# Four moves in the order of work of a fused attention and mixer kernel: k.v split about its denominators, blocks closed in pairs, w2's loads behind another event, S4 earlier

## The chip, the cores and the metric

The kernel runs on one core of one Trainium2 chip. The metric is the device time of an execution in microseconds (us); the median of three runs before the change is 292.44 us, from 292.41 to 292.49.

The engines are called as the profile calls them: PE is TensorE's matmuls and PEld its weight loads, DVE is VectorE, ACT is ScalarE, POOL is GpSimd and SP is SyncE, which issues most DMA transfers. L684 is line 684 of the kernel before the change.

## What is computed

Cosine-weighted linear attention over 8 batches, 8 heads, 576 tokens of 64 features, and behind it a mixer over tokens of rank 32 and a two-layer perceptron over channels (512 to 2048 to 512).

```python
q_p, k_p = phi(q), phi(k)               # relu, times cos and sin of the position: 128 features
kv = einsum('bhsf,bhsd->bhfd', k_p, v)
z = sum(k_p, axis=2)
x = einsum('bhsf,bhfd->bhsd', q_p, kv) / (einsum('bhsf,bhf->bhs', q_p, z) + 1e-6)
# x goes to (batch, token, 512)
u = x + ((x.T @ U) @ V).T               # U: 576 x 32, V: 32 x 576
out = u + relu(u @ w_ch1) @ w_ch2
```

## The kernel before

**Tiles.** The 576 tokens of a batch are four chunks of 128 (c = 0 to 3) and a tail of 64 (c = 4); the tails of two batches share one tile of 128 rows. All products run in bf16 and add up in PSUM in fp32. PSUM's banks go by tags that rotate: "g" has three (`G3` in the code), "T" (`T1`) and the pair "oA", "oB" one each, "X" a double one.

**Order.** The order is written by hand: each engine has one queue of instructions, in the order in which the program emits them, and an instruction that waits holds back all that is behind it on its engine. Batch 0's attention comes first, by functions of its own. Behind it stands a list of slots (`lay`, `lay_all`): each is one unit of TensorE work of some 0.9 us, and `beside` and `todo` put thunks behind given slots (other engines' work, the attention of the next batch, loads). For an even and an odd batch in turn the slots are 16 units of the first product (`first_units`: u @ w_ch1 and relu) and then the second product; batch 0's second product is 16 plain units (`g2_part`, L755), the others' are 14 half steps (`second_units`, `w_part`).

**Batch 0's attention.** q's chunks are turned into features by DVE and ACT (`q_prep`, L307 and L305), transposed on TensorE (`qtr_mm`, L386, into the three "g" banks and oA, oB) and copied to `q_pT` (`qtr_evac`, L114 on ACT and L116 on DVE): chunk 0 by DVE, 1 by ACT, 3 and the tail by ACT later. Chunk 2 is copied by DVE inside `first_chain`. k's features follow (`k_prep`), with their sums z as products with ones (`z_mm`, L1178). Then `first_chain` (L1232 to L1282):

- DVE casts v into `v0` in two casts of two heads and one of four, casts z into `z_sb`, and copies q^T's chunk 2 between them.
- `kv_unit(b, 0)` (L341) multiplies heads 0 to 3 (20 products) into a "g" bank; ACT evacuates them to `kv_sb`. Then `den_mm` (L1186): 40 products of 12 columns give the denominators of all chunks; DVE adds 1e-6 and takes the reciprocal (L421, L422).
- `xh_mm` (L1194) gives x before division for a chunk's four heads, `xh_norm` (L1203, DVE) and `xh_norm_act` (L1226, ACT) divide. The second four heads follow `kv_unit(b, 1)`.
- `a_mm` (L457) is x.T @ U for two of the four blocks of 128 channels at a time, in column groups of 32; it reads `x_of(b, c)` of all five chunks. A cast puts it into `A_sb`.
- u^T, block by block: `open_mm` (L1217) transposes x's four chunks into a bank, and `uTd_mm` (L557) "closes" it by adding A times V, one product of 512 columns on a row group of 32. `uTd_evac` casts it to `uT`. Blocks 0 and 1 are opened and closed one after the other; blocks 2 and 3 behind the second `a_mm`, with two of batch 0's first-layer products ahead of their closing (`g1_open`, L701) and four behind.

**Loads.** SP issues q, k and v of the next batches in order, behind one-element copies that hold it until something is done. POOL issues w_ch1 in four loads, then a copy `mark` that reads a piece of batch 1's k (L1326) and so waits until it has landed, then w_ch2 in four (L108). SP's `gate` on w2's second load (L1341) stands ahead of batch 2's loads. Batch 1's k.v (L341, slots 16 and 17) reads casts of v that DVE makes in slots 14 and 15 (`v_half`).

**Second product of batches 1 to 7.** It is done by seven block products instead of eight, with sums of blocks of w2 (`T`) and of the relu output (`S1`, `S2`, `S3`, `S4`; `hid_form`, L830, each in two halves). `w_part(b, n)` is half step n: 8 pairs of products on one of four banks. Steps in order of n / 2: 0 plain, 1 with S2, 2 with S1, 3 with S3, 4 plain, 5 with S4 (into the bank of step 2), 6 plain. The second halves of S1 and S2 are made behind half step 0, S3's behind 2, S4's behind 4. After odd half steps, DVE and POOL take the banks up (L874): behind step 1, DVE adds it to `w_sum`, DVE makes one piece of the output tile `o_sb` and POOL two more; behind steps 2 to 6, DVE adds the bank to its piece.

Of the kernel before, what the change touches and what calls it, by code (L numbers as in the profile page):

```python
# [10 lines left out]
FP32 = mybir.dt.float32  # L11
BF16 = mybir.dt.bfloat16
# [5 lines left out]
def kernel(  # L18
# [93 lines left out]
    def cast(eng, o, i):  # L112
        if eng is nc.scalar:
            nc.scalar.activation(out=o, in_=i, func=AF.Copy, bias=0.0, scale=1.0)  # L114
        else:
            eng.tensor_copy(out=o, in_=i)  # L116
# [216 lines left out]
    def kv_unit(b, hg, tag, bufs, eng=None):  # L333
        if b not in kv_sb:
            kv_sb[b] = pool.tile([P, H, E], BF16, tag="kv", bufs=2, name="kv")
        n = D if b == 0 else E
        acc = bank([P, 4, n], FP32, tag, bufs, "kv_ps")
        for i in range(4):
            h = hg * 4 + i
            for c in range(5):  # L340
                nc.tensor.matmul(  # L341
                    out=acc[:, i, :],
                    lhsT=k_p[b][:, c, h, :] if c < 4 else k_tl[:, h, :],
                    rhs=v0[:, h, c, :] if b == 0 else vx_of(b, c, h),
                    start=(c == 0),
                    stop=(c == 4),
                )
        cast(eng or V_, kv_sb[b][:, hg * 4 : hg * 4 + 4, 0:n], acc)

    def kv_pair(b, tag, bufs):  # L350
        kv_sb[b] = pool.tile([P, H, E], BF16, tag="kv", bufs=2, name="kv")
# [39 lines left out]
    def qtr_evac(b, c, eng, t):  # L391
        if c < 4:
            cast(eng, q_pT[b][:, c, :, :], t)
        else:
            cast(eng, q_tlT[:, :, tail(b)], t[:, :, 0:P:2])
# [156 lines left out]
    def uTd_evac(b, d, eng):  # L552
        cast(eng, uT[b][:, d, :, :], uT_ps[b, d])
# [289 lines left out]
    def w_part(b, n):  # L843
        step, half = divmod(n, 2)
        lhs, rhs, to = (
            (lambda: hid_block(b, 0, 0), w2_block(0, 0), 0),
            (lambda: s_forms[b, 2], T[1], 1),
            (lambda: s_forms[b, 1], T[0], 2),
            (lambda: s_forms[b, 3], T[2], 3),
            (lambda: hid_block(b, 1, 0), w2_block(1, 0), 0),  # L850
            (lambda: s_forms[b, 4], w2_block(1, 1), 2),
            (lambda: hid_block(b, 1, 1), T[3], 3),
        )[step]
        lhs = lhs()
        opens = step < 4
        if opens and half == 0:
            tag, bufs = T1 if to == 0 else G3
            w_ps[to] = bank([P, DM], FP32, tag, bufs, f"w_ps{to}")
        res = w_ps[to].rearrange("p (g n) -> p g n", g=2)
        for k_ in range(half * 4, half * 4 + 4):  # L860
            for g in range(2):
                nc.tensor.matmul(  # L862
                    out=res[:, g, :], lhsT=lhs[:, k_, g * P : g * P + P], rhs=rhs[:, k_, :],
                    start=(opens and k_ == 0 and g == 0),
                    stop=(k_ == KB - 1 and g == 1), skip_group_check=not opens,
                )
        for f in ({0: (4,), 2: (3,)} if b == B - 1 else {0: (1, 2), 2: (3,), 4: (4,)}).get(n, ()):
            hid_form(b, f, 1)
        if half == 0:
            return  # L870
        lo, hi = slice(0, HD), slice(HD, DM)

        def add(eng, o, x, y):
            eng.tensor_tensor(out=o, in0=x, in1=y, op=ALU.add)  # L874

        def by_d(t):
            return t.rearrange("p c (d n) -> p d c n", n=P)

        def u(c0, h):
            return u_bf[b][:, 2 * h : 2 * h + 2, c0 : c0 + 2, :]  # L880

        if step == 0:
            w_sum[b] = pool.tile([P, 2, HD], FP32, tag="w_sum", bufs=1, name="w_sum")
            cast(A_, w_sum[b], res)
        elif step == 1:
            w = w_sum[b]
            o0, o1 = o_alloc(b, 0), o_alloc(b, 1)
            add(V_, w, w, res)
            add(V_, by_d(o1[:, :, hi]), by_d(w), u(2, 1))
            add(G_, by_d(o0[:, :, hi]), by_d(w), u(0, 1))  # L890
            add(G_, by_d(o1[:, :, lo]), by_d(w), u(2, 0))
        elif step == 2 or step == 3:
            o = o_sb[b, 1][:, :, hi]
            add(V_, o, o, res)
        elif step == 4:
            add(V_, by_d(o_sb[b, 0][:, :, lo]), u(0, 0), by_d(res))
        elif step == 5:
            o = o_sb[b, 0][:, :, hi]
            add(V_, o, o, res)
            store_w(b, 0, 0)  # L900
        else:
            o = o_sb[b, 1][:, :, lo]
            add(V_, o, o, res)
            store_w(b, 2, 1)
# [278 lines left out]
    def den_mm(b, d, cs):  # L1183
        for c in cs:
            for h in range(H):
                nc.tensor.matmul(  # L1186
                    out=d[:, c, h, :], lhsT=qT_of(b, c, h),
                    rhs=z_sb[:, h : h + 1].to_broadcast([P, 12]), start=True, stop=True,
                )
# [25 lines left out]
    def open_mm(b, d, t, cs):  # L1215
        for c in cs:
            nc.tensor.matmul(  # L1217
                out=t[:, c, :], lhsT=x_bf[b][:, c, d * P : d * P + P], rhs=ident,
                start=(c == 0), stop=False,
            )  # L1220
# [11 lines left out]
    def first_chain(b, xz, z, v_ps):  # L1232
# [6 lines left out]

        d = xz[:, 1, 0:480].rearrange("p (c h n) -> p c h n", h=H, n=12)  # L1240
        rec = pool.tile([P, 5, H], FP32, tag="rec5", bufs=1, name="rec5")
        for h in (0, 2):
            cast(V_, v0[:, h : h + 2], vst[:, h : h + 2])
        cast(V_, z_sb, z[:, :, 0])
        qtr_evac(b, 2, V_, t_q[2])
        cast(V_, v0[:, 4:H], vst[:, 4:H])
        qtr_evac(b, 4, A_, t_q[4])
        kv_unit(b, 0, *G3, A_)
        cast(A_, V_bf, v_ps.rearrange("r (c p) -> r c p", c=4))
        den_mm(b, d, (0, 1, 3, 2, 4))  # L1250
        recip(rec, d[:, :, :, 0])
        x0 = [xh_mm(b, c, 0, *G3) for c in ORD[0:2]]
        kv_unit(b, 1, *T1, A_)
# [10 lines left out]
        cast(A_, A_of(b)[0:TS, :], a_ps[0:TS, :])  # L1264
        for i, (tag, bufs) in enumerate((OA, OB, T1)):
            uT_ps[b, i] = bank([P, 4, P], FP32, tag, bufs, "uT_ps")
        open_mm(b, 0, uT_ps[b, 0], range(4))
        x1.append(xh_mm(b, ORD[4], 4, *G3))
        for n in range(2, 5):
            xh_norm(b, ORD[n], 4, rec, x1[n])  # L1270
        uTd_mm(b, 0)
        uTd_evac(b, 0, A_)
        open_mm(b, 1, uT_ps[b, 1], range(4))
        uTd_mm(b, 1)
        uTd_evac(b, 1, A_)
        a2 = bank([P, P], FP32, *G3, "a_ps")
        a_mm(b, a2, (2, 3), range(5))
        cast(V_, A_of(b)[TS:P, :], a2[TS:P, :])
# [14 lines left out]
    for c in TL:  # L1293
        q_prep(0, c, FEATS[c])
        qtr_mm(0, c, 0, H, t_q[c])
        keep_warm(1, "X", 1)
    for c, eng in zip(TL[0:2], (V_, A_)):
        qtr_evac(0, c, eng, t_q[c])
    xz = ps.tile([P, 2, 512], FP32, tag="X", bufs=1, name="xz")
    z = xz[:, 0, 0:384].rearrange("p (h n) -> p h n", n=48)  # L1300
# [22 lines left out]
    for h0 in (0, 4):  # L1323
        load_odd(vst, v, 1, h0, h0 + 4)
        load_even(vst, v, 1, h0, h0 + 4)
    G_.tensor_copy(out=mark, in_=kst[0:TS, 3, 4, 0:1])  # L1326
    for n in range(4):
        w2_load(n)
    g1_open(0, (0, 0), (0, 1))
    uTd_close(0, 2, V_)  # L1330
    uTd_close(0, 3, A_)
    g1_open(0, (0, 2), (1, 0), (1, 1), (1, 2))
    q_prep(1, 4, (V_, A_))
    q_prep(1, 0, (V_, V_))


    def at(j, *thunks):
        beside.setdefault(j, []).extend(thunks)

    def gate(src):  # L1340
        nc.sync.dma_start(out=mark2, in_=src)  # L1341
# [102 lines left out]
```

## Time and profile before

| | us |
|---|---|
| median of three runs | 292.44 (292.41 to 292.49) |
| the profiled execution | 292.46 |
| its span, first to last instruction | 290.7 |
| PE busy | 285.7 |
| DVE busy | 224.5 |
| ACT busy | 162.2 |
| POOL busy | 67.5 |

The span is what the trace shows; 1.76 us of the profiled execution lie outside it. The ends of matmuls are modelled from their pipeline, so they overlap, and PE's busy time is above what its work needs. The granted TensorE clock was 1.0 throughout. The timeline's rows give start, length, engine, line, operation, output<-inputs, shapes and the count that is merged; a bracket gives the idle time of the engine ahead and what ended it.

### The profile page before, as it was taken

To read this page: it belongs to the slowest core of one execution; us is meant where nothing else is said; L and a number is where in the kernel's file an instruction comes from. 1 tells how busy PE (TensorE), PEld (TensorE's weight loads), DVE (VectorE), ACT (ScalarE), POOL (GpSimd) and SP (SyncE) were. 2 spreads that over 40 slices of the span, in tenths; PEclk is the share of its full clock that TensorE was granted. 3 is DMA by queue.
4 is the path that set the end of the run, shared out by engine and by line. 5 is a ranking of instruction groups with operands and counts; after the bars stand their busy time and mean duration, and the time that the engine had idled before them with its cause. 6 is when DMAs were issued, how large, how long until landed. Compare 5 with 4: busy or idle time off the path is not lost.

```text
span 290.7 us, 7417 instructions
## 1 busy us (share of the span) xinstructions
PE 285.7 (98%) x3062; PEld 206.0 (71%) x3062; DVE 224.5 (77%) x447; ACT 162.2 (56%) x282; POOL 67.5 (23%) x104
## 2 busy tenths in 40 slices
PE   8999999999999999999999999999999999999995
PEld 6876455545987546876986646876888548999884
DVE  4879748887898778948896377848899687769974
ACT  2965651576593456966693456966791562067100
POOL 8340500050052303640042500441031102100210
PEclk9999999999999999999999999999999999999999
DMA  6999999999939999799838995999186304120023
GB/s 200 337 283 253 261 186 264 297 245 221 287 86 153 231 357 194 216 278 265 237 58 181 229 281 100 249 249 291 18 145 77 148 12 81 49 99 0 2 87 132
DMA packets 85447, 53.32 MB, mean 183 GB/s; under 512 B 53990, under 2 KB 83078, under 8 KB 85414
## 3 DMA queue, kind: packets, MB, share of 16 engines
q1 hardware_dynamic: 78998, 41.62, 60.5%
q0 software_dynamic: 6272, 11.17, 15.8%
q8 instruction: 24, 0.39, 0.6%
q14 instruction: 9, 0.07, 0.1%
q10 hardware_dynamic: 144, 0.07, 0.1%
HBM read 36.86 MB, written 9.44 MB: 159 GB/s over the span
## 4 chain that ended last, share of the span: by engine, by line
PE 96%; DVE 2%; issue 1%; DVEq 0%
PE g_ps L684 29%; PE w_ps L862 28%; PE gt_ps L715 5%; PE o_ps L755 5%; PE al_ps L635 5%; PE be_ps L635 4%; PE w_ps L202 3%; PE x_ps L431 3%; PE kv_ps L356 2%; PE ot_ps L775 2%; PE ot_ps L963 2%; PE a_ps L457 1%; PE va_ps L487 1%; DVE u_bf L498 1%; PE t_ps L374 1%; PE t_ps L386 1%
## 5 line engine op out<-in xcount | busy, mean ns | idle before, releaser
L684 PE MATMUL g_ps<-uT,w_bf 128*128 128x512 bf16 x378 | 91.2, 379 | 0.0
L691 ACT ACTIVATE hid<-g_ps 128x512 bf16<-128x512 f32 x96 | 57.0, 597 | 44.6 <-PE g_ps L684 37.6
L684 PEld LDWEIGHTS <-w_bf 128*128 128x128 bf16 x378 | 34.3, 98 | 33.5
L874 POOL TENSOR_TENSOR o_sb<-w_sum,u_bf 128x512 f32<-128x512 f32 x14 | 22.1, 1595 | 117.5 <-DVE w_sum L874 117.5
L862 PEld LDWEIGHTS <-hid 128*128 128x128 bf16 x448 | 43.6, 98 | 5.6
L862 PEld LDWEIGHTS <-S 128*128 128x128 bf16 x336 | 32.3, 98 | 4.9 <-issue 0.5
L862 PE MATMUL w_ps<-T,hid 128*128 128x256 bf16 x224 | 26.9, 273 | 0.0
L862 PE MATMUL w_ps<-w_bf,hid 128*128 128x256 bf16 x224 | 26.9, 273 | 0.0
L862 PE MATMUL w_ps<-T,S 128*128 128x256 bf16 x224 | 26.3, 273 | 0.0
L652 DVE TENSOR_TENSOR hid<-pw,be_ps 128x512 bf16<-128x512 f32 x24 | 16.4, 685 | 11.9 <-ACT pw L114 7.6
L114 ACT ACTIVATE pw<-al_ps 128x512 f32<-128x512 f32 x24 | 14.2, 597 | 18.2 <-PE al_ps L635 17.4
L874 DVE TENSOR_TENSOR o_sb<-o_sb,w_ps 128x512 f32<-128x512 f32 x28 | 19.1, 682 | 4.9 <-PE w_ps L862 4.3
L498 DVE TENSOR_TENSOR u_bf<-x_bf,va_ps 128x1024 bf16<-128x1024 bf16 (+1 forms) x20 | 19.5, 1001 | 4.0 <-PE va_ps L487 3.9
L441 DVE TENSOR_TENSOR x_bf<-x_ps,rec 128x512 bf16<-128x512 f32 x28 | 19.3, 691 | 1.0
L305 ACT ACTIVATE k_p<-kst,sinw 128x512 bf16<-128x512 f32 x26 | 17.7, 712 | 0.0
L729 POOL DMA_DIRECT2D out_dram<-o_sb x12 | 7.6, 632 | 41.2 <-DVE o_sb L763 20.9
L116 POOL CAST v_ext<-vst 128x512 bf16<-128x512 f32 x24 | 15.6, 694 | 6.1 <-issue 3.7
L715 PE MATMUL gt_ps<-uT_tl,w_bf 128*128 128x128 bf16 x256 | 16.4, 219 | 0.0
L755 PE MATMUL o_ps<-w_bf,hid 128*128 128x512 bf16 x64 | 15.6, 379 | 0.0
L830 DVE TENSOR_TENSOR S<-hid,S 128x1024 bf16<-128x1024 bf16 x14 | 15.4, 1097 | 0.1
L715 PEld LDWEIGHTS <-w_bf 128*128 128x128 bf16 x256 | 15.0, 98 | 0.4
L305 ACT ACTIVATE q_p<-qst,cosw 128x512 bf16<-128x512 f32 x21 | 14.4, 712 | 0.0
(188 smaller groups left out, 472.7 us busy)
## 6 DMA issues: line engine op xcount, KB each, us to landing
qst<-in_q_dram SPq DMA_DIRECT2D x14, 512.0 KB, 6.3
kst<-in_k_dram SPq DMA_DIRECT2D x14, 512.0 KB, 8.2
vst<-in_v_dram SPq DMA_DIRECT2D x12, 512.0 KB, 7.9
out_dram<-o_sb POOLq DMA_DIRECT2D x12, 512.0 KB, 5.2
w_bf<-in_moe_w_ch_dram POOLq DMA_DIRECT2D x8, 512.0 KB, 10.2
out_dram<-o_sb SPq DMA_DIRECT2D x4, 512.0 KB, 3.0
qst<-in_q_dram SPq DMA_DIRECT2D x2, 640.0 KB, 5.8
kst<-in_k_dram SPq DMA_DIRECT2D x2, 640.0 KB, 13.8
```

Of the source, the lines that this page charges most:

```text
L116: eng.tensor_copy(out=o, in_=i)
L305: nc.scalar.activation(out=o, in_=i, func=AF.Relu, bias=0.0, scale=w)
L441: nc.vector.tensor_tensor(out=x_of(b, c, rows).rearrange("p (g i d) -> p g i d", g=2, d=D), in0=view[:, :, :, 0:D], in1=rec[rows].unsqueez ...
L498: nc.vector.tensor_tensor(out=u_bf[b][:, d0 : d0 + n], in0=x_bf[b].rearrange("p c (d n) -> p d c n", n=P)[:, d0 : d0 + n], in1=t.rearrange ...
L635: nc.tensor.matmul(out=res[:, k_, :], lhsT=lhs[:, d, k_, :], rhs=rhs[:, d, :], start=(opens and k_ == 0 and d == 0), stop=(k_ == 1 and d = ...
L652: V_.tensor_tensor(out=o, in0=x, in1=res, op=ALU.add)
L684: nc.tensor.matmul(out=g_ps.rearrange("p (c t) -> p c t", c=4), lhsT=w1_bf[:, d, j * P : j * P + P], rhs=uT[b][:, d, :, :], start=(d == 0) ...
L691: nc.scalar.activation(out=hid[b][:, j, :], in_=g_ps, func=AF.Relu, bias=0.0, scale=1.0)
L715: nc.tensor.matmul(out=g_ps[:, jj, :], lhsT=w1_bf[:, d, j * P : j * P + P], rhs=uT_tl[pr][:, d, :], start=(d == 0), stop=(d == 3),)
L755: nc.tensor.matmul(out=o, lhsT=hid[0][:, j, cc * P : cc * P + P], rhs=w2_bf[:, j, :], start=(j == 0), stop=(j == NJ - 1),)
L862: nc.tensor.matmul(out=res[:, g, :], lhsT=lhs[:, k_, g * P : g * P + P], rhs=rhs[:, k_, :], start=(opens and k_ == 0 and g == 0), stop=(k_ ...
L874: eng.tensor_tensor(out=o, in0=x, in1=y, op=ALU.add)
```

## The change

Four parts, all of order:

1. **k.v about the denominators.** DVE copies q^T's chunk 2 ahead of k's features. `first_chain` casts two heads of v, then z, then the rest of v. The first half of k.v is no longer `kv_unit`: heads 0 and 1, denominators of chunks 0 to 2, heads 2 and 3, denominators of 3 and 4. ACT casts V ahead of k.v's evacuation instead of behind it.
2. **Pairs.** u^T's blocks 0 and 1 are both opened ahead of the last `xh_mm`, and closed one directly behind the other; blocks 2 and 3 are closed ahead of all six `g1_open` products.
3. **w2.** POOL's `mark` ahead of w2's loads reads batch 1's q^T (chunk 3, copied by DVE behind slot 5) and not batch 1's k; it and the loads are emitted behind slot 6.
4. **S4.** `hid_form(b, 4, 1)` behind half step 1 instead of 4, for batches 1 to 6.

```diff
+    def kv0_mm(b, acc, hs):
+        for h in hs:
+            for c in range(5):
+                nc.tensor.matmul(
+                    out=acc[:, h, :], lhsT=k_p[b][:, c, h, :] if c < 4 else k_tl[:, h, :],
+                    rhs=v0[:, h, c, :], start=(c == 0), stop=(c == 4),
+                )
...
-        for f in ({0: (4,), 2: (3,)} if b == B - 1 else {0: (1, 2), 2: (3,), 4: (4,)}).get(n, ()):
+        for f in ({0: (4,), 2: (3,)} if b == B - 1 else {0: (1, 2), 1: (4,), 2: (3,)}).get(n, ()):
...
-        for h in (0, 2):
-            cast(V_, v0[:, h : h + 2], vst[:, h : h + 2])
+        cast(V_, v0[:, 0:2], vst[:, 0:2])
         cast(V_, z_sb, z[:, :, 0])
-        qtr_evac(b, 2, V_, t_q[2])
+        cast(V_, v0[:, 2:4], vst[:, 2:4])
         cast(V_, v0[:, 4:H], vst[:, 4:H])
         qtr_evac(b, 4, A_, t_q[4])
-        kv_unit(b, 0, *G3, A_)
+        kv_sb[b] = pool.tile([P, H, E], BF16, tag="kv", bufs=2, name="kv")
+        acc = bank([P, 4, D], FP32, *G3, "kv_ps")
+        kv0_mm(b, acc, (0, 1))
+        den_mm(b, d, (0, 1, 2))
+        kv0_mm(b, acc, (2, 3))
         cast(A_, V_bf, v_ps.rearrange("r (c p) -> r c p", c=4))
-        den_mm(b, d, (0, 1, 3, 2, 4))
+        cast(A_, kv_sb[b][:, 0:4, 0:D], acc)
+        den_mm(b, d, (3, 4))
...
-        open_mm(b, 0, uT_ps[b, 0], range(4))
+        for i in range(2):
+            open_mm(b, i, uT_ps[b, i], range(4))
         x1.append(xh_mm(b, ORD[4], 4, *G3))
         for n in range(2, 5):
             xh_norm(b, ORD[n], 4, rec, x1[n])
-        uTd_mm(b, 0)
-        uTd_evac(b, 0, A_)
-        open_mm(b, 1, uT_ps[b, 1], range(4))
-        uTd_mm(b, 1)
-        uTd_evac(b, 1, A_)
+        for i in range(2):
+            uTd_mm(b, i)
+        for i in range(2):
+            uTd_evac(b, i, A_)
...
-    for c, eng in zip(TL[0:2], (V_, A_)):
+    for c, eng in zip(TL[0:3], (V_, A_, V_)):
         qtr_evac(0, c, eng, t_q[c])
...
-    G_.tensor_copy(out=mark, in_=kst[0:TS, 3, 4, 0:1])
-    for n in range(4):
-        w2_load(n)
-    g1_open(0, (0, 0), (0, 1))
-    uTd_close(0, 2, V_)
-    uTd_close(0, 3, A_)
-    g1_open(0, (0, 2), (1, 0), (1, 1), (1, 2))
+    for d in (2, 3):
+        uTd_mm(0, d)
+    uTd_evac(0, 2, V_)
+    uTd_evac(0, 3, A_)
+    g1_open(0, *((d, j) for d in range(2) for j in range(3)))
...
+    def w2_all():
+        G_.tensor_copy(out=mark[0:1], in_=q_pT[1][0:1, 3, 0, 0:1])
+        for n in range(4):
+            w2_load(n)
+
+    at(6, w2_all)
```

## The prediction

> **What bounds the kernel now.** I read the page first: the span, then the chain that ended last. A row of the timeline below is start, length, engine, line, operation, output<-inputs, count, and in brackets the idle time ahead of it. A matmul's length holds its pipeline, so TensorE's pace is read from start to start.
>
> ```profile
> span 290.7 us, 7417 instructions
> ...
> PE 96%; DVE 2%; issue 1%; DVEq 0%
> ```
>
> TensorE is on the chain nearly all the time, so a change counts only where TensorE waits. Following the chain through time, I find three such places: batch 0's attention (to about 23 us) and one step each of the second products of batches 3 and 5. Those two first.
>
> ```profile
> 142.03 0.68 DVE L830 TENSOR_TENSOR S<-hid,S 128x1024 bf16<-128x1024 bf16 x1
> ...
> 149.68 3.23 POOL L874 TENSOR_TENSOR o_sb<-w_sum,u_bf 128x512 f32<-128x512 f32 x2 [18.34 <-DVE w_sum L874]
> ...
> 150.24 1.65 DVE L830 TENSOR_TENSOR S<-hid,S 128x1024 bf16<-128x1024 bf16 x1
> ...
> 151.65 1.91 PE L862 MATMUL w_ps<-w_bf,hid 128*128 128x256 bf16 x16
> ...
> 153.00 1.47 DVE L874 TENSOR_TENSOR o_sb<-o_sb,w_ps 128x512 f32<-128x512 f32 x2
> ...
> 153.73 1.91 PE L862 MATMUL w_ps<-w_bf,S 128*128 128x256 bf16 x16 [0.17 <-DVE o_sb L874]
> ...
> 155.47 1.91 PE L862 MATMUL w_ps<-T,hid 128*128 128x256 bf16 x16
> ```
>
> A step of 16 products takes 1.74 us to the next (155.47 - 153.73), but from 151.65 to 153.73 it is 2.08: **0.34 us lost**, though the bracket says 0.17. The S4 step (153.73) adds into the bank that the first o_sb addition of 153.00 reads, so it waits for that one. Ahead of that addition DVE has spent 1.65 us on S4's second half, which elsewhere (142.03) takes 0.68. Batch 5 shows the same:
>
> ```profile
> 216.06 1.65 DVE L830 TENSOR_TENSOR S<-hid,S 128x1024 bf16<-128x1024 bf16 x1
> ...
> 217.63 1.91 PE L862 MATMUL w_ps<-w_bf,hid 128*128 128x256 bf16 x16
> ...
> 218.83 0.67 DVE L874 TENSOR_TENSOR o_sb<-o_sb,w_ps 128x512 f32<-128x512 f32 x1
> ...
> 219.56 1.91 PE L862 MATMUL w_ps<-w_bf,S 128*128 128x256 bf16 x16
> ```
>
> 219.56 - 217.63 is 1.93, so **0.19 us lost**. The addition ends at 219.50 and releases TensorE. In batches 1, 2, 4 and 6 the chain runs through these steps without a pause.
>
> **S4's second half two half steps sooner.** Nothing is added; one DVE instruction per batch moves ahead of S3's second half, the w_sum addition and the additions behind it. In the new place (about 146.2 us in batch 3) POOL is idle: its row of 149.68 has 18.34 us of idle time ahead. So I take the undisturbed 0.60 us to the next start (0.68 long). Then u_bf, w_sum and POOL's two additions start 0.6 us later, and the waited-for addition starts 0.6 later less the 1.57 us of the old place: 152.0 instead of 153.0, done at 152.7. TensorE wants it at 151.65 + 1.74 = 153.39: the 0.34 us go, with 0.7 to spare. In batch 5 the same shift ends the addition near 218.5, wanted at 219.37: the 0.19 us go. Gain 0.53 us; bounds 0 (S4 as long in its new place) and 0.53, as these two waits are all there is. S3's second half, now behind S4, is wanted six half steps (5 us) after the product starts; it is pushed 0.6 us, or 1.6 if S4 is slowed there too.
>
> Here a rule of the Trainium skill bears: "SBUF — State Buffer", Who interferes with whom, says that a DVE instruction with two SBUF inputs is shut out entirely while a GpSimd instruction that reads SBUF runs. Two additions in 3.23 us make the first end near 151.3; 0.6 more is 151.9, where the row of 150.24 ends, so the trace agrees. By the rule, any other two-input instruction that comes to stand behind those additions pays instead; those that do (u_bf, o_sb) read one input from PSUM, so the sum stands. If instead S4 were slow wherever it stood, 0 of the 0.53 would come.
>
> **u^T's blocks closed in pairs.**
>
> ```profile
> 19.02 0.40 PE L1217 MATMUL uT_ps<-ident,x_bf 128*128 128x128 bf16 x4
> 19.25 0.29 PE L1194 MATMUL xh_ps<-kv,q_pT 128*128 128x64 bf16 x4
> 19.47 0.38 PE L557 MATMUL uT_ps<-V_bf,A_sb 32*128 32x512 bf16 x1
> 19.79 0.40 PE L1217 MATMUL uT_ps<-ident,x_bf 128*128 128x128 bf16 x4
> 20.12 0.39 PE L557 MATMUL uT_ps<-V_bf,A_sb 32*128 32x512 bf16 x1
> 20.43 0.40 PE L457 MATMUL a_ps<-x_bf,U_bf 128*32 128x128 bf16 x8
> 20.67 0.22 PE L457 MATMUL a_ps<-x_tl,U_bf 128*32 128x128 bf16 x2
> ...
> 21.81 0.39 PE L557 MATMUL uT_ps<-V_bf,A_sb 32*128 32x512 bf16 x1
> 21.81 0.38 PE L557 MATMUL u<-V_bf,A_sb 32*128 32x512 bf16 x1
> 22.13 1.04 PE L701 MATMUL g_ps<-uT,w_bf 128*128 128x512 bf16 x4
> ```
>
> A close (L557) alone costs 0.32 us to the next start (19.47 to 19.79, 20.12 to 20.43), two on different row groups 0.32 together (21.81 to 22.13); about 0.1 of it, and 0.1 ahead, is the change between a 32-row and a full matmul. Now blocks 0 and 1 open together (19.02, 19.25, to 19.48), the xh group follows (to 19.60), and after 0.1 both closes go at 19.70; the a_ps group could start at 20.02 instead of 20.43. But it needs DVE's last x_bf, so the gain is cut there:
>
> ```profile
> 18.82 1.40 DVE L1203 TENSOR_TENSOR x_bf<-xh_ps,rec 128x256 bf16<-128x256 f32 x4
> ```
>
> These end at 20.22; a_ps's fourth chunk goes 0.05 later and the tail's pair (20.67 now) near 20.33: gain 0.34. What follows keeps its distances: blocks 2 and 3 still close in a pair between two changes, only the two L701 products that stood ahead now stand behind. ACT's two evacuations follow the pair: 0.6 us each (the V_bf row below has their shape) from 20.1 to 21.4, and block 1's products come three products behind block 0's, near 22.0.
>
> **Batch 0's k.v split about its denominators.** This part sets how much later those x_bf come.
>
> ```profile
> 10.79 0.33 PE L386 MATMUL t_ps<-ident,q_p 128*128 128x128 bf16 x3
> ...
> 11.48 1.28 DVE L307 TENSOR_SCALAR k_p<-kst,cosw 128x512 bf16<-128x512 f32 x3 [0.71 <-DMA kst<-in_k_dram]
> ...
> 14.60 0.28 PE L341 MATMUL kv_ps<-v,k_p 128*128 128x64 bf16 x4
> ...
> 14.79 0.17 DVE L116 CAST z_sb<-xz 128x8 bf16<-128x8 f32 x1
> 14.87 0.68 DVE L116 COPY q_pT<-t_ps 128x1024 bf16<-128x1024 bf16 x1
> ...
> 15.18 0.95 PE L1186 MATMUL xz<-z_sb,q_pT 128*128 128x12 bf16 x32
> ...
> 15.66 0.59 ACT L114 ACTIVATE V_bf<-v_ps 128x512 bf16<-128x512 f32 x1
> ...
> 16.24 0.28 PE L1194 MATMUL xh_ps<-kv,q_tlT 128*128 128x64 bf16 x4
> ```
>
> The q_pT copy of chunk 2 moves from 14.87 into the idle 0.71 us before 11.48. Its transposes end at 11.12 (10.79 + 0.33), so it runs 11.16 to 11.84; the next DVE instruction starts 0.60 behind its start, at 11.76, and DVE's k features come 0.28 us later. I take it that TensorE's products wait for them no longer than now, so z keeps its time; the first v0 cast ends 0.28 later, about 14.6, and k.v's first two heads, at 14.60 now, start up to 0.1 late. The second v0 cast is behind z (14.87 to about 15.4). Denominators 0 to 2 start when z_sb is out (15.0). One of the 40 takes 0.026 (15.18 to 16.24), one of k.v's 20 takes 0.029 (14.60 to 15.18): 24 x 0.026 + 10 x 0.029 + 16 x 0.026 = 1.33: the end is near 16.3 instead of 16.24. So rec, and with it every x_bf, comes 0.05 later: the 0.34 above becomes 0.29, and I take **0.30 us** for both parts. The evacuation of k.v's four heads now stands behind V_bf (15.66, 0.59 long) and behind heads 2 and 3, about 16.1 to 16.5, and puts the first xh 0.28 later, at 16.52; DVE reads it only behind rec and its reciprocal. Bounds: -0.25 (if xh's 0.28 falls on the norms in full and pairing gives next to nothing) and 0.41 (all of 20.43 to 20.02).
>
> **w2 behind batch 1's q^T.**
>
> ```profile
> 29.32 0.69 DVE L116 COPY q_pT<-t_ps 128x1024 bf16<-128x1024 bf16 x1 [0.45 <-PE t_ps L374]
> ...
> 38.86 1.03 PE L755 MATMUL o_ps<-w_bf,hid 128*128 128x512 bf16 x4
> ```
> ```profile
> L108 POOL DMA_DIRECT2D w_bf<-in_moe_w_ch_dram x1: 745/745/745, 32.3 to 32.3; - x1
> ...
> DMA to landing us min/median/max: 6.3/6.3/6.3
> ```
>
> The first w2 load lands at 32.3 + 6.3 = 38.6; its first reader starts at 38.86. So without this edit some 0.1 of the 0.30 us would be eaten. POOL's mark now waits for the copy that ends at 30.0 (29.7 after the gain) instead of k's landing, so POOL issues the four loads from about 30.2, and SP's gate on the second one opens some 2 us sooner for batch 2's loads. Behind the mark on POOL are the four V_qt copies, which only move ahead. Cost taken: 0; the price if it isn't is the third rival's.
>
> **Sum.** 0.53 + 0.30 = 0.83 us off. The profiled execution took 292.46 us, 1.76 outside its span; the median is 292.44. 292.44 - 0.83 = **291.61 us**.
>
> **The rivals.**
> *The start gives nothing* (0.18): the norm chain is later than I worked out, by xh or by the k features, and only S4's 0.53 comes: 291.9. For it: DVE feeds this stage almost without idle time. Against it: the norms queue on DVE, so an xh 0.28 later has their queue to hide behind.
> *S4 gives nothing* (0.05): the addition is late for another reason; only 0.30 comes: 292.14. Against it: DVE shows no other gap in that stretch.
> *Batch 1's v lands late* (0.15, of it 0.07 on the slow side). w2 used to wait until k was in; now it moves beside v.
>
> ```profile
> L74 SPq DMA_DIRECT2D vst<-in_v_dram x2: 1527/1848/2170, 19.3 to 22.8; - x2
> ...
> DMA to landing us min/median/max: 12.7/14.6/14.7
> ```
> ```profile
> 37.51 0.68 DVE L116 CAST v_ext<-vst 128x1024 bf16<-128x1024 f32 x1
> ...
> 41.19 0.28 PE L341 MATMUL kv_ps<-v_ext,k_p 128*128 128x65 bf16 x4
> ```
>
> The last v load lands at 22.8 + 12.7 = 35.5, and w2's packets may come from 32 on. Shared evenly, v's last 2 to 3.5 us become 4 to 7: landing at 37.5 to 39. Its casts take about 1 us, and TensorE reads them near 40.7 (first row of that group, less 0.3): the point is a landing at 39.6. Each us beyond it is a us of TensorE: with a landing at 41.2 the whole is 0.8 slower, 293.2. What makes it so is w2 getting two thirds of the engines or more, or all: w2 first would put v up to 10 us off. The Trainium skill, "DMA: Bandwidth & Descriptors", Queues, rings and completion order, has each DMA engine take turns between its queues packet by packet; by an even turn v would land near 38, and the sum stays. The page's GB/s don't part the queues, so this trace doesn't test it.
>
> **How the numbers follow.** My forecast 0.57 (291.45 to 291.8); more than that, as the start gives up to 0.41 or a later small wait goes, 0.05; the rivals as above. The range 291.4 to 292.15 takes in the first two rivals and half of the third. A measurement tells about 0.2% (0.58 us) from no change. Faster than that needs 291.86: the forecast, the 0.05 above it and part of the first rival, 0.67; within it the rest of the first rival, the second and half of the third, 0.25; slower 0.08, the rest of the third and what I don't see.
>
> **What would show it.** In the changed profile: L830's longest S at 0.7 in batches 3 and 5, and 1.75 us from step to step there; the blocks' closes in two pairs, the a_ps tail near 20.4 and the first products that follow 0.3 sooner; w2's first landing before 38.5; no idle DVE ahead of v_ext, or if so none on TensorE at L341. I am wrong if the 0.3 us at 23 us are gone by 42 us, or if the norms end later than 20.35.

## The result and the profile after

The changed kernel takes 291.82 us (median of 13 runs, 291.55 to 292.93), the kernel before 292.56 beside it (13 runs, from 292.40): a ratio of 0.9972, 95% interval 0.996 to 0.9983. The profiled execution took 291.72 us with a span of 289.9; it was 292.46 and 290.7. So the median is 0.74 us lower and the span 0.8 shorter, where 0.83 were forecast. Medians count every run; one run each of the kernel before, of S4 alone, of w1's loads sooner and of the cast on ScalarE was in a slower state of the chip, and moves its median by at most 0.14 us.

Medians of this kernel carry waits that change from execution to execution (they are named below), so the experiments quote the lowest run beside the median: 292.40 before and 291.55 after, a difference of 0.85. The lowest run of the kernel before is 292.20 to 292.40 by chip and occasion, so a difference between lowest runs from two of these is good to some 0.2 us. Lines below L350 have their numbers; behind it they stand 8 to 17 further down (L830 is now L838, L874 L882, L862 L870, L684 L692, L701 L709, L557 L565, L1186 L1194, L1194 L1202, L1203 L1211, L457 L465, L755 L763).

**The second products.** The timeline of the changed kernel in batch 3, with rows of DVE, POOL and PE in order of time:

```profile
145.91 0.69 DVE L838 TENSOR_TENSOR S<-hid,S 128x1024 bf16<-128x1024 bf16 x1
...
149.81 2.78 POOL L882 TENSOR_TENSOR o_sb<-w_sum,u_bf 128x512 f32<-128x512 f32 x2 [18.78 <-DVE w_sum L882]
...
151.34 1.91 PE L870 MATMUL w_ps<-w_bf,hid 128*128 128x256 bf16 x16
...
151.56 1.47 DVE L882 TENSOR_TENSOR o_sb<-o_sb,w_ps 128x512 f32<-128x512 f32 x2
...
153.09 1.91 PE L870 MATMUL w_ps<-w_bf,S 128*128 128x256 bf16 x16
...
154.84 1.91 PE L870 MATMUL w_ps<-T,hid 128*128 128x256 bf16 x16
```

S4 takes 0.69 in its new place, the waited-for addition starts at 151.56 instead of 153.00, and the step takes 1.75 (153.09 - 151.34) instead of 2.08. POOL's two additions have become shorter too, 2.78 instead of 3.23. In batch 5 the same step is 1.75 instead of 1.93:

```profile
216.99 1.91 PE L870 MATMUL w_ps<-w_bf,hid 128*128 128x256 bf16 x16
218.74 1.91 PE L870 MATMUL w_ps<-w_bf,S 128*128 128x256 bf16 x16
```

In the view of S's source line no instruction is longer than 0.69 us, over all batches (columns: count, shortest/median/longest in ns):

```profile
L838 DVE TENSOR_TENSOR S<-hid,S x14: 676/684/693, 73.8 to 271.5; 128x1024 bf16<-128x1024 bf16 x14
```

**The start.** PE's timeline, then DVE's with one row of ACT's:

```profile
19.04 0.62 PE L1225 MATMUL uT_ps<-ident,x_bf 128*128 128x128 bf16 x8
19.50 0.29 PE L1202 MATMUL xh_ps<-kv,q_pT 128*128 128x64 bf16 x4
19.72 0.39 PE L565 MATMUL uT_ps<-V_bf,A_sb 32*128 32x512 bf16 x2
20.04 0.50 PE L465 MATMUL a_ps<-x_bf,U_bf 128*32 128x128 bf16 x8
20.36 0.23 PE L465 MATMUL a_ps<-x_tl,U_bf 128*32 128x128 bf16 x2
...
22.70 1.03 PE L692 MATMUL g_ps<-uT,w_bf 128*128 128x512 bf16 x4
```
```profile
11.10 2.56 ACT L305 ACTIVATE k_p<-kst,sinw 128x512 bf16<-128x512 f32 x4
11.37 1.26 DVE L307 TENSOR_SCALAR k_p<-kst,cosw 128x512 bf16<-128x512 f32 x3
...
15.70 0.83 DVE L116 CAST v<-vst 128x1280 bf16<-128x1280 f32 x1 [0.78 <-DMA vst<-in_v_dram]
16.45 0.19 DVE L429 TENSOR_SCALAR rec<-xz 128x40 f32<-128x40 f32 x1
...
17.18 0.42 DVE L1211 TENSOR_TENSOR x_tl<-xh_ps,rec 64x256 bf16<-64x256 f32 x1
...
18.85 1.40 DVE L1211 TENSOR_TENSOR x_bf<-xh_ps,rec 128x256 bf16<-128x256 f32 x4
```

The two closes take one place (19.72 to 20.04), the a_ps tail goes at 20.36 instead of 20.67, and the products that follow start at 22.70 instead of 23.00: 0.30. The norms end where they did, at 20.25 (20.22). But two things ahead of them changed. k landed at 11.01 instead of 11.39: ACT's first k feature starts at 11.10, DVE's only at 11.37, when the copy of q^T's chunk 2 is done. And DVE had to wait 0.78 us for v ahead of `rec`, which the trace of before doesn't show. The trace reports each load in sixteen parts, and a load has landed with the last: fifteen parts of this one were there by 14.27, the last came at 15.61.

**w2.** POOL's issues, by source line, and the first reader:

```profile
L108 POOL DMA_DIRECT2D w_bf<-in_moe_w_ch_dram x4: 747/756/770, 30.3 to 32.5; - x4
...
DMA to landing us min/median/max: 7.9/10.6/13.4
```
```profile
38.56 0.81 PE L763 MATMUL o_ps<-w_bf,hid 128*128 128x512 bf16 x3
```

The issue comes 2.0 us sooner (30.3 for 32.3), the first landing only 0.5 (30.3 + 7.9 = 38.2 for 38.7). The reader starts 0.30 sooner, so the gain of the start is kept.

### The profile page after: what moved, and what is told of

It is laid out like the page before. It is cut to its first block, busy times and chain, and to the rows that moved or that the text cites. A ratio compares the mean times of both kernels' runs of the same rounds, so it can differ in the third digit from the quotient of the medians.

```text
span 289.9 us, 7392 instructions
## 1 busy us (share of the span) xinstructions
PE 283.2 (98%) x3036; PEld 205.3 (71%) x3062; DVE 219.1 (76%) x447; ACT 162.1 (56%) x282; POOL 66.4 (23%) x104
## 4 chain that ended last, share of the span: by engine, by line
PE 92%; DMA 3%; DVE 2%; issue 1%; SPq 0%; DVEq 0%
PE w_ps L870 30%; PE g_ps L692 28%; PE al_ps L643 5%; PE gt_ps L723 5%; PE o_ps L763 5%; PE be_ps L643 4%; DMA vst<-in_v_dram 3%; PE x_ps L439 3%; PE kv_ps L364 3%; PE ot_ps L783 2%; PE ot_ps L971 2%; PE a_ps L465 1%; PE va_ps L495 1%; PE t_ps L382 1%; PE va_ps L518 0%
## 5 line engine op out<-in xcount | busy, mean ns | idle before, releaser
L692 PE MATMUL g_ps<-uT,w_bf 128*128 128x512 bf16 x361 | 89.5, 379 | 0.7
L692 PEld LDWEIGHTS <-w_bf 128*128 128x128 bf16 x378 | 34.3, 98 | 33.6
L870 PEld LDWEIGHTS <-hid 128*128 128x128 bf16 x448 | 43.6, 98 | 5.6
L882 POOL TENSOR_TENSOR o_sb<-w_sum,u_bf 128x512 f32<-128x512 f32 x14 | 19.5, 1410 | 120.4 <-DVE w_sum L882 120.4
L870 PEld LDWEIGHTS <-S 128*128 128x128 bf16 x336 | 32.4, 98 | 4.3
L870 PE MATMUL w_ps<-T,hid 128*128 128x256 bf16 x224 | 26.9, 273 | 0.0
L870 PE MATMUL w_ps<-w_bf,hid 128*128 128x256 bf16 x224 | 26.9, 273 | 0.0
L870 PE MATMUL w_ps<-T,S 128*128 128x256 bf16 x224 | 26.3, 273 | 0.0
L882 DVE TENSOR_TENSOR o_sb<-o_sb,w_ps 128x512 f32<-128x512 f32 x28 | 19.2, 685 | 8.2 <-PE w_ps L870 7.8
L116 POOL CAST v_ext<-vst 128x512 bf16<-128x512 f32 x24 | 17.2, 756 | 5.8 <-issue 3.7
L763 PE MATMUL o_ps<-w_bf,hid 128*128 128x512 bf16 x61 | 15.3, 379 | 0.2
L429 DVE TENSOR_SCALAR rec<-x_ps 128x8 f32<-128x8 f32 (+1 forms) x35 | 5.7, 163 | 10.9 <-PE x_ps L439 10.5
```

The costliest lines, as they stand in the source:

```text
L692: nc.tensor.matmul(out=g_ps.rearrange("p (c t) -> p c t", c=4), lhsT=w1_bf[:, d, j * P : j * P + P], rhs=uT[b][:, d, :, :], start=(d == 0) ...
L763: nc.tensor.matmul(out=o, lhsT=hid[0][:, j, cc * P : cc * P + P], rhs=w2_bf[:, j, :], start=(j == 0), stop=(j == NJ - 1),)
L870: nc.tensor.matmul(out=res[:, g, :], lhsT=lhs[:, k_, g * P : g * P + P], rhs=rhs[:, k_, :], start=(opens and k_ == 0 and g == 0), stop=(k_ ...
```

## The experiments

Each kernel has 12 runs if nothing else is said, beside 27 to 35 of the kernel before on its chip.

### S4 alone

```diff
-... {0: (1, 2), 2: (3,), 4: (4,)}
+... {0: (1, 2), 1: (4,), 2: (3,)}
```

> The kernel before with the S4 move alone. Theory: POOL's two additions hold S4's second half up (1.65 us instead of 0.68), so it stands ahead of them at 0.7 in every batch, the two late steps (0.34 us in batch 3, 0.19 in batch 5) are back at 1.75 us from start to start, nothing else moves: 0.53 us less, near 291.9. Rival (another instruction comes to stand behind POOL's additions and pays instead, or the addition is late for another reason): a late step stays in batch 3 or 5, 0 to 0.2 us less.

Measured: 292.22 us, ratio 0.9981 (0.9965 to 0.9996); lowest 291.87, 0.53 under the lowest before. No S over 0.693 us, and the steps in batches 3 and 5 take 1.75. The profiled execution took 293.06, more than before, and the waits of that profile say why: TensorE stood still for 0.84 us ahead of the first o_ps, which the S4 edit doesn't touch (the eleven products from 36.78, at 0.215 each, were over at 39.15).

```profile
36.78 2.54 PE L684 MATMUL g_ps<-uT,w_bf 128*128 128x512 bf16 x11
39.99 1.02 PE L755 MATMUL o_ps<-w_bf,hid 128*128 128x512 bf16 x4 [0.67 <-DMA w_bf<-in_moe_w_ch_dram]
```

S4's term is 0.53 by the lowest runs, as forecast, and the two late steps of the trace account for it; the time of one profiled execution would have hidden it.

### The pairs alone

```diff
-        open_mm(b, 0, ...)
+        for i in range(2): open_mm(b, i, ...)
...
-        uTd_mm(b, 0) ... open_mm(b, 1, ...) ... uTd_mm(b, 1)
+        for i in range(2): uTd_mm(b, i)
...
-    g1_open(0, (0, 0), (0, 1))
-    uTd_close(0, 2, V_)
-    uTd_close(0, 3, A_)
+    for d in (2, 3): uTd_mm(0, d)
```

> The kernel before with u^T's blocks closed in pairs, alone. Theory: the a_ps tail's pair comes near 20.33 instead of 20.67 and the first full product behind the blocks 0.34 us sooner; the first second-layer product then waits some 0.1 us for w2's first load (landing near 38.6), so 0.2 to 0.25 us less in all, near 292.25. Rival (the start's gain is the k.v split's, or is the chance of when q and k land): a_ps's tail not below 20.55 counted from the same start of k's features, nothing in time.

Measured: 292.69 us, ratio 0.9994 (0.9978 to 1.001); lowest 292.07, 0.33 under the lowest before. PE's timeline:

```profile
19.74 0.39 PE L557 MATMUL uT_ps<-V_bf,A_sb 32*128 32x512 bf16 x2
...
20.38 0.23 PE L457 MATMUL a_ps<-x_tl,U_bf 128*32 128x128 bf16 x2
...
22.73 1.03 PE L684 MATMUL g_ps<-uT,w_bf 128*128 128x512 bf16 x4
```

The tail follows the last norm (20.27) by 0.11; before by 0.45 (20.67 - 20.22). In these profiles all the gain of the start is in this edit. The wait of 0.1 us for w2 that was expected didn't come: w2 landed at 38.43 and its reader started at 38.58. S4's late step is still there:

```profile
151.37 1.91 PE L862 MATMUL w_ps<-w_bf,hid 128*128 128x256 bf16 x16
153.44 1.91 PE L862 MATMUL w_ps<-w_bf,S 128*128 128x256 bf16 x16 [0.17 <-DVE o_sb L874]
```

The median doesn't show the 0.33; its interval is wider than that.

### k.v's split alone, and everything but the split

```diff
-        kv_unit(b, 0, *G3, A_)
-        den_mm(b, d, (0, 1, 3, 2, 4))
+        kv0_mm(b, acc, (0, 1))
+        den_mm(b, d, (0, 1, 2))
+        kv0_mm(b, acc, (2, 3))
+        den_mm(b, d, (3, 4))
```

The casts of v, z and q^T's chunk 2 go with it, as in the change.

> The kernel before with k.v split about the denominators (and q^T's chunk 2 copied ahead of k's features), alone. Theory: the denominators end 0.05 us later than before, the norms with them, so no gain: 0 to 0.1 us more, near 292.5. Rival (this part made the gain at the start): the norms end 0.2 to 0.3 us sooner than 20.22, and 0.2 to 0.3 us less in all.

> The changed kernel without the k.v split (pairs, w2 and S4 stay). Theory: as fast as the changed kernel or 0.05 us faster, 0.8 to 0.9 us below the kernel before, near 291.6. Rival (the split made the gain at the start): 0.2 to 0.3 us slower than the changed kernel, 0.5 below the kernel before.

Measured: the split alone 293.00 us, ratio 1.0001 (0.9982 to 1.002), lowest 292.43 (0.03 above). Everything but the split 291.93, ratio 0.9979 (0.9962 to 0.9996), lowest 291.59 (0.04 above the whole change). So the split gives nothing that can be measured. The lowest runs add up: 0.53 (S4) + 0.33 (pairs) - 0.03 (split) = 0.83, against 0.85 for all. That they agree to 0.02 is in part luck: where the changed kernel was run again the whole change is 0.69 (292.20, 291.51) and 0.86 (292.30, 291.44). The medians add up less well, 0.61 + 0.14 - 0.17 = 0.58 against 0.74, and they hold w2's waits as well.

Why it gives nothing is seen from all the profiles together. Times from the span's start: first k feature on DVE, start of the last v0 cast, end of the denominators (taken as the start of the weight load behind them), start of `rec`, end of the norms, a_ps tail.

| kernel | split | k | last v cast | denominators | rec | norms' end | a_ps tail |
|---|---|---|---|---|---|---|---|
| before | no | 11.48 | 15.47 | 16.21 | 16.42 | 20.22 | 20.67 |
| pairs alone | no | 11.54 | 15.40 | 16.25 | 16.46 | 20.27 | 20.38 |
| all but the split | no | 11.87 | 15.73 | 16.46 | 16.67 | 20.48 | 20.59 |
| split alone | yes | 12.03 | 15.52 | 16.53 | 16.73 | 20.54 | 21.02 |
| change without w2 (below) | yes | 11.34 | 14.85 | 15.96 | 16.17 | 19.98 | 20.09 |
| change | yes | 11.37 | 15.70, waits 0.78 | 16.02 | 16.45 | 20.25 | 20.36 |
| change, second profile | yes | 11.43 | 16.18, waits 1.17 | 15.93 | 16.92 | 20.73 | 20.84 |
| change, third profile | yes | 12.24 | 15.74 | 16.74 | 16.95 | 20.79 | 20.90 |

Without the split `rec` comes 4.80 to 4.94 us behind the first k feature on DVE. With it, it comes 4.70 to 4.83 behind, if v is there. But where k is early this count flatters the split, because the copy that now stands ahead of k holds DVE's first k feature up. Counted from k's landing, the three kernels without the split and with a late k (11.78 to 11.93; S4 alone and the half step below are the other two) have `rec` 4.89 behind, and the two with the split (11.93, 12.15) 4.80: 0.09 sooner. With an early k it is 5.02 and 5.03 without the split (11.44, 11.39), and 5.05 and 5.07 with it where the copy held DVE's first k feature up by 0.14 and 0.27 against ACT's (the change without w2 and the halves of the last experiment): nothing is gained. Where v is late, `rec` comes 0.74 behind the start of the last v cast, which stands ahead of it in DVE's queue in both orders. That was so in the first two profiles of the change, where v's last part came at 15.61 and 16.09; in all others it came at 14.37 to 15.32. So the split takes 0.1 off where neither the copy nor v is in the way, and nothing elsewhere. The a_ps tail is 0.11 behind the norms in each kernel with pairs and 0.44 to 0.48 in each without.

### The w2 edit undone

```diff
+    G_.tensor_copy(out=mark, in_=kst[0:TS, 3, 4, 0:1])
+    for n in range(4):
+        w2_load(n)
...
-    at(6, w2_all)
```

> The changed kernel with the w2 edit undone: the four w2 loads stand again behind the mark on k's landing, so POOL issues them near 32.3 us instead of 30.3. Theory of the prediction: without this edit about 0.1 us of the start's gain is eaten, because w2's first load lands near 38.6 and its reader is ready at 38.56; the kernel stands 0.1 us above the changed kernel run beside it. Rival theory, from the five traces so far: w2's first load lands 5.1 to 5.3 us behind w1's fourth load whatever its own issue, so its landing stays at w1's fourth plus 5.2 (with w1's fourth at 33.0, 38.2) and the time stays within 0.05 us of the changed kernel; only w2's later loads land 1 to 2 us later, for which nothing waits.

Measured: 292.07 us, ratio 0.9974 (0.9958 to 0.999), lowest 291.65. The changed kernel on the same chip: 291.73, ratio 0.9965 (0.9949 to 0.9981), lowest 291.51. So w2's edit is worth 0.14 by the lowest runs and 0.34 by the medians, and the intervals of the two ratios overlap. The profile of the kernel without it shows the price, by source line and on PE:

```profile
L108 POOL DMA_DIRECT2D w_bf<-in_moe_w_ch_dram x4: 745/755/770, 32.1 to 34.3; - x4
...
DMA to landing us min/median/max: 6.9/10.5/13.6
```
```profile
36.78 1.67 PE L692 MATMUL g_ps<-uT,w_bf 128*128 128x512 bf16 x7
39.01 1.02 PE L763 MATMUL o_ps<-w_bf,hid 128*128 128x512 bf16 x4 [0.56 <-DMA w_bf<-in_moe_w_ch_dram]
```

w2 lands at 39.0 (32.1 + 6.9), and the seven products from 36.78 at 0.215 each were over at 38.3: 0.7 us lost, more than the start had gained. The rival expectation (the landing follows w1's fourth load by 5.2 us whatever its issue) falls in part: here it is 5.5 behind (33.46 to 38.97). The profiles of kernels whose other loads and whose v casts stand as in the change or before it, with the landings of w1's fourth and w2's first load and what TensorE lost ahead of the first o_ps:

| kernel | mark | w2 issued | w1's fourth | w2's first | between | lost |
|---|---|---|---|---|---|---|
| before | old | 32.34 | 33.04 | 38.69 | 5.65 | 0 |
| pairs alone | old | 32.25 | 33.29 | 38.43 | 5.14 | 0 |
| change without w2 | old | 32.08 | 33.46 | 38.97 | 5.51 | 0.72 |
| S4 alone | old | 32.34 | 34.66 | 39.95 | 5.29 | 0.84 |
| split alone | old | 32.50 | 35.28 | 40.47 | 5.19 | 1.31 |
| S4 one half step sooner (below) | old | 32.96 | 35.87 | 40.37 | 4.50 | 1.03 |
| change | new | 30.30 | 33.01 | 38.19 | 5.18 | 0 |
| all but the split | new | 30.53 | 33.66 | 38.85 | 5.19 | 0.10 |
| change, second | new | 30.78 | 34.30 | 39.01 | 4.71 | 0.02 |
| change, third | new | 30.84 | 34.56 | 39.20 | 4.64 | 0.14 |

With the old mark four of six lose 0.7 to 1.3 us; with the new one none of these four loses more than 0.14, and the four kernels further below lose nothing. Most of that is w1's own landing, which came as late as 35.87 with the old mark and no later than 34.56 with the new one, and the time at which TensorE is ready. At an equal landing of w1's fourth the new mark is 0.75 ahead at 34.6 (39.95 against 39.20) and 0.5 at 33.0. In between, the pairs alone (33.29 to 38.43) do as well as the new mark's neighbours (33.01 to 38.19, 33.66 to 38.85). So the gain of w2's edit in time is not clear of the noise, and no run here parts it from the chance of w1's landing.

The sixteen parts tell more than the landing. The eighth part of w2's first load came at 37.44 to 38.21 in the six rows with the old mark and at 36.36 to 37.04 in the four with the new one, 1.20 sooner in the change than before (36.54, 37.74). So the load does follow its issue. But the last part came 0.8 to 2.7 us behind the eighth, as that of w1's fourth load came 1.5 to 4.0 behind its eighth, and TensorE waits for the last. Why a few parts come so late stays open.

### S4 one half step sooner only

```diff
-... {0: (1, 2), 2: (3,), 4: (4,)}
+... {0: (1, 2), 2: (3,), 3: (4,)}
```

> The kernel before with S4's second half one half step sooner only, just ahead of the w_sum addition but behind S3's second half and still ahead of the waited-for o_sb addition. Theory (POOL's two additions shut S4 out): S4 comes before POOL begins, takes 0.7 us, both late steps go and the fastest run stands 0.53 us under the fastest before, as in the run with the whole S4 edit. Rival (the place in DVE's queue itself counts: S4 must be two half steps ahead): the late steps stay, wholly or in part, and the gain is under 0.3 us. No S over 0.75 us by the theory; 1.0 or more by the rival.

Measured: 292.25 us, ratio 0.9986 (0.9966 to 1.0005), lowest 291.87, the same as with the whole S4 edit. But the kernel before reaches down to 292.20 in its 35 runs there, 292.40 in the 35 beside the whole edit, so by the lowest runs the gain is 0.33 and not the expected 0.53. What decides is the trace, here DVE, POOL and PE in batch 3:

```profile
150.47 0.68 DVE L830 TENSOR_TENSOR S<-hid,S 128x1024 bf16<-128x1024 bf16 x1
151.07 0.68 DVE L874 TENSOR_TENSOR w_sum<-w_sum,w_ps 128x512 f32<-128x512 f32 x1
```
```profile
151.84 2.77 POOL L874 TENSOR_TENSOR o_sb<-w_sum,u_bf 128x512 f32<-128x512 f32 x2 [18.95 <-DVE w_sum L874]
```
```profile
153.21 1.91 PE L862 MATMUL w_ps<-w_bf,hid 128*128 128x256 bf16 x16
154.95 1.91 PE L862 MATMUL w_ps<-w_bf,S 128*128 128x256 bf16 x16
```

S4 still stands ahead of the waited-for addition, four instructions later than in the change, but ahead of POOL's two: 0.68 long, the step 1.74. In batch 5 the step is 1.75 (218.85 to 220.60). What cost the two late steps their 0.53 was running S4 beside POOL's additions, not how far ahead in DVE's queue it stands. It agrees with the rule of the Trainium skill that the prediction weighed ("SBUF — State Buffer", Who interferes with whom). The numbers are S4's 0.68 and POOL's 2.77 apart against 1.65 and 3.23 together, while the two u_bf of one input from PSUM take 1.27 us beside POOL's additions in both kernels.

### w1's loads sooner, and the changed kernel beside it

```diff
-    G_.tensor_copy(out=mark[0:1], in_=q_tlT[0:1, 0, 0:1])
+    G_.tensor_copy(out=mark[0:1], in_=k_p[0][0:1, 3, 0, 0:1])
     for n in range(1, 4):
         w1_load(n)
```

> The changed kernel with the mark ahead of w1's loads 2 to 4 on batch 0's k features (ready near 13.8 us) instead of the tail's q^T (15.0): the three loads are issued about 1.4 us sooner. Theory (w2's first load follows w1's fourth by 5.2 us, and its landing beside the o_ps product decides the spread of the executions): w1's fourth lands 0.5 to 1.4 us sooner, w2's first as well, no execution waits for w2 at the first o_ps; the fastest run is the changed kernel's, the median comes 0.1 to 0.3 us nearer to it. Rival (the loads share the engines with batch 1's q, which lands at 20.7 and is needed near 22): q lands up to 1 us later and the first transposes of batch 1's q come late, so the kernel is 0 to 0.5 us slower than the changed one.

> The changed kernel again, beside the three other runs on their chip: 291.55 us in its fastest run, a median 0.6 to 0.85 us under the kernel before; a second profile of it shows whether the 0.3 us at the start are still there behind the first o_ps when w1's loads land at another time.

Measured: 292.76 us, ratio 0.9993 (0.9974 to 1.0012), lowest 291.62; the changed kernel beside it 291.73, 0.9965 (0.9949 to 0.9981). The median is 1.0 us worse, the lowest run 0.1. The theory fails, and what its rival named happens, by more than the rival put it. Issued 0.9 us or more sooner than in any profile of the changed kernel, w1's fourth load lands at 33.69, within that kernel's 33.01 to 34.56. But batch 1's q lands at 24.1 (20.7, 22.4 and 20.8 in the three profiles of the changed kernel): two of its sixteen parts come at 23.02 and 24.09, the others by 20.02. That the earlier loads made these two late is argued from one profile and the median. PE's timeline shows who waits:

```profile
24.95 0.62 PE L382 MATMUL t_ps<-ident,q_tl 128*128 128x128 bf16 x8 [0.80 <-ACT q_tl L305]
```

The second profile of the changed kernel has the later `rec` of the table above (16.92), its norms, closes and first products 0.48 later than in the first, and keeps all of S4's gain.

### The last v cast on ScalarE, w2's first load in halves

```diff
-        cast(V_, v0[:, 4:H], vst[:, 4:H])
...
         cast(A_, kv_sb[b][:, 0:4, 0:D], acc)
+        cast(A_, v0[:, 4:H], vst[:, 4:H])
```

> The changed kernel with the cast of batch 0's last four v heads taken from VectorE (where rec, the reciprocal and all norms queue behind it) and given to ScalarE behind k.v's first evacuation. Theory (what k.v's split gains is lost in most executions because that cast waits for v, 0.78 us in the first profile of the changed kernel and 1.17 in the second): rec starts at the end of the denominators, near 16.1 us, whenever v lands; the first norm comes near 16.9 instead of 17.2 to 17.7. The second four heads' xh then come later by ScalarE's queue (the cast about 1.1 us, so k.v's second evacuation near 17.9), and the last norm ends near 20.3: the fastest run is within 0.15 us of the changed kernel's, and executions with a late v gain up to 0.4. Rival (ScalarE is the dearer place: its norm of the fifth chunk and a_ps's first evacuation queue behind the cast): closes 0.3 to 0.4 us later, the kernel 0.2 to 0.4 us slower than the changed one.

```diff
-        for n in range(4):
+        for lo in (0, 2):
+            w2_load(0, lo, lo + 2)
+        for n in range(1, 4):
             w2_load(n)
```

> The changed kernel with w2's first load cut in two of half the rows, the order and the mark unchanged, so that the first two of the four o_ps products can be served sooner. Theory (the first o_ps is held by w2's first landing in executions with late w1 loads, and the landing is a matter of bytes behind w1's fourth): the first half lands 0.5 to 1 us sooner than the whole, about 4.5 us behind w1's fourth load; waits at the first o_ps shrink by up to 0.4 us, the fastest run stays at 291.5 to 291.6. Rival (the landing is a fixed delay behind w1 and not bytes, or the fifth issue costs as much as it gains): the first half lands 5.0 to 5.3 us behind w1's fourth, the time stays or gets 0.1 worse.

> The two edits together (the last v cast on ScalarE, w2's first load in halves). If the start gains 0.1 to 0.3 us and w2's first half lands by 38.2, the fastest run is 291.3 to 291.5 and the median under the changed kernel's. If ScalarE's queue eats the gain, it stands 0.1 to 0.4 us above the changed kernel; if only w2 holds, it stays at 291.55.

> The changed kernel once more as a yardstick beside the three on their chip: 291.5 to 291.6 us in its fastest run, 0.6 to 0.85 us under the kernel before in the median. By the reading of the two profiles so far its norms start 0.7 to 0.75 us behind the end of the last v cast's wait, and w2's first load lands 4.7 to 5.3 us behind w1's fourth.

Measured, on one chip (12, 8, 12 and 8 runs): the cast on ScalarE 292.51 us, ratio 0.9984 (0.9968 to 1.0), lowest 292.05; the halves 291.69, 0.9945 (0.9914 to 0.9976), lowest 291.30; both 292.45, 0.9986 (0.9966 to 1.0006); the changed kernel 291.62, 0.9952 (0.9932 to 0.9972), lowest 291.44.

The cast on ScalarE costs 0.6 us by the lowest runs and 0.9 by the medians instead of gaining; with both edits it is 0.65 and 0.8, more than any of the cases that had been expected. `rec` does come at 16.30, behind the denominators alone, but the cast takes 1.26 us there, k.v's second half starts at 17.29 (16.59 in the change), and now the norms wait for xh:

```profile
16.30 0.20 DVE L429 TENSOR_SCALAR rec<-xz 128x40 f32<-128x40 f32 x1 [1.35 <-PE xz L1194]
...
18.20 0.76 DVE L1211 TENSOR_TENSOR x_bf<-xh_ps,rec 128x256 bf16<-128x256 f32 x2 [0.41 <-PE xh_ps L1202]
```

They end at 20.84. The rival expectation named the right engine; the wait is ahead of the norms rather than of the closes.

In halves w2's first rows land sooner, as the theory of bytes had it and by more than its 4.5: 3.3 and 3.6 us behind w1's fourth (33.77 to 37.04; 34.27 to 37.87), and neither profile has a wait at the first o_ps. By the time the halves and the changed kernel can't be told apart (291.69 and 291.62): with the new mark at most 0.14 was left to win there in any profile. That the lowest run of all, 291.30, is the halves' is one run of eight. The changed kernel itself was 1.2 us under the kernel before by the medians beside each other on that chip, where 0.6 to 0.85 had been expected: the kernel before stood at 292.83 there.

## Why the prediction was right, step by step

**S4: right in place, cause and size.** 0.53 forecast, 0.53 between the lowest runs with S4 alone and before, and both late steps are 1.75 in each trace where S4 was moved. The addition was expected near 152.0 on before's time axis; it is at 151.56, on an axis that runs 0.3 ahead. Not foreseen: POOL's pair got 0.45 shorter, so S4 and the additions had slowed each other.

**The pairs: right.** 0.34 forecast, cut by the last x_bf; the tail went from 0.45 to 0.11 behind the norms, 0.34, and the lowest run by 0.33.

**The split: the right number by luck.** Norms 0.05 later were forecast; they are 0.02 later in the first profile, and 0.5 later in the second and third (20.73, 20.79), beyond the 20.35 that the prediction named as its sign of being wrong. The copy of q^T's chunk 2 ran from 10.77 and not from 11.16, so DVE was free for k at 11.37, ahead of before's 11.48. In this execution k had landed 0.38 sooner, and the copy did hold DVE's first k feature up, by 0.27 against ACT's (11.10). z_sb came at 14.36 instead of 14.79, as the last of z's products came that much sooner (14.14, 14.57 before). And the denominators ended at 16.02 instead of the forecast 16.3. What took that back is a wait that the prediction didn't list: the last v cast, in DVE's queue ahead of `rec`, waits for v. An early k and a late v happened to cancel. The rival "the start gives nothing" named the norm chain, but by xh or k; neither was late, and that rival's condition didn't come true.

**w2: right in direction, the size too small.** "Some 0.1" of the start's gain was said to be at stake. That holds for the execution that was profiled before, where w2 landed 0.17 ahead of its reader. In other executions w1's fourth load lands up to 2.8 us later (35.87) and w2's first up to 1.8 (40.47), and TensorE then loses 0.7 to 1.3 us. The forecast for the median used one execution's margin. And the gate on w2's second load opened 1.1 us sooner and not 2: batch 2's first load is issued at 41.47 instead of 42.6.

**The rival "batch 1's v lands late": its range was right, its point not reached.** In the first profile after, v lands at 36.6 and nothing waits; in the second DVE waits for it:

```profile
38.13 0.69 DVE L116 CAST v_ext<-vst 128x1024 bf16<-128x1024 f32 x1 [1.02 <-DMA vst<-in_v_dram]
```

The landings in five profiles with the new mark and w2's loads whole or halved (change, all but the split, second, third, halves) are 36.6, 37.9, 38.0, 38.3 and 37.7; in two kernels whose loads or casts were moved it was 36.2 (w1 sooner) and 35.4 (cast on ScalarE). 37.5 to 39 had been worked out, and a stall of TensorE from 39.6 on (by the prediction's own row the reader starts at 41.19 - 0.3 = 40.9 and not 40.7, so the point is 39.8). The latest, with both edits of the last experiment, was 39.33, and DVE waited 1.98 us, but k.v's second half starts at 41.70 there and lost nothing. In the five, v's last load lands 3.6 to 4.3 us behind w1's fourth, in the other three with the new mark 2.4, 2.5 and 5.1, with the old mark 1.9 to 2.4: what w2 gains by its early issue v pays, out of slack. But it is not the whole load that is slowed, as the prediction had it. The eighth of v's sixteen parts comes at 33.97 to 34.52 in the five and at 33.91 to 34.81 with the old mark; only the last parts are later. The Trainium skill's even turn between queues ("DMA: Bandwidth & Descriptors", Queues, rings and completion order) would put v near 38; four of the five landings are there, but with the old mark and a late w1 one is too (38.20), so no run here tests it.

The other rivals: S4 gave all it could; the 0.3 us at 23 us were still there at 38.56, and at 40.89, where k.v's second half starts (41.19 before).

## What to carry to other kernels

Where an engine's instruction takes 1.65 us in one place and 0.68 in all others, look at what another engine does in that stretch, and move it ahead of that; one half step was enough here. Before crediting a reordering of one engine's queue, list each transfer that something in that queue still waits for: here the last part of v set `rec` in two of three profiles of the change, by a cast that the reordering had left ahead of it. And take the margin of a landing from several executions: the profile of before showed w2 in time by 0.17 us, in other kernels with the same mark w2 missed its reader by up to 1.3.

## What the runs showed of the hardware

- S4 and POOL's two additions slowed each other where they overlapped: S4 took 1.65 us beside them and 0.69 away from them, the two additions 3.23 and 2.78.
- A load is reported in sixteen parts, and its landing is the last of them: of batch 0's last v load fifteen came by 14.27 and one at 15.61, and DVE waited 0.78 us for it.
- w2's loads stand behind w1's on one queue. Issued 2 us sooner, half of the first load's parts were there 1.20 us sooner, the last only 0.5. Its landing was 4.5 to 5.65 us behind w1's fourth with the old mark and 4.6 to 5.2 with the new one; with half the rows 3.3 and 3.6.
- Three of w1's loads issued 0.9 us or more sooner landed no sooner than the spread of the others (the fourth at 33.69; 33.01 to 34.56), and in that profile another queue's load (q) landed 1.7 to 3.4 us later, by two of its sixteen parts.
- The same cast of 1280 columns takes 0.83 us on DVE and 1.26 on ACT.
